# Decoding float64 weights in five vector operations, phi's maxima chunk by chunk, and a new plan table

## The chip, the cores and the metric

The kernel runs on one core of one Trainium2 chip. A core has five engines that run side by side, each with its own instruction list: PE (TensorE, matrix products into PSUM), DVE (VectorE), ACT (ScalarE), POOL (GpSimd) and SP (SyncE, which here only issues DMAs). The metric is the device time of one execution in microseconds (us).

## The reference

Attention with memory slots, then a feed-forward layer, all in float32:

```python
a = softmax(phi over the sequence)          # phi: 8 batches, 8 heads, 576 tokens, 32 slots
k_m = einsum('bhsm,bhsd->bhmd', a, k)       # keys and values gathered into the slots
v_m = einsum('bhsm,bhsd->bhmd', a, v)
attn = softmax(q @ k_m.T / 8 over the slots)
x = attn @ v_m                              # 4608 tokens x 512
h = x @ w_in                                # w_in 512 x 2048, w_out 2048 x 512
out = relu(h)**2 @ w_out
```

w_in and w_out arrive as float64, two 32-bit words for each number. The engines work in float32, so each weight has to be rebuilt from its words ("decoded").

## The kernel before, in words

**Products.** Every float32 product is made of several products of the rounded type fp32r: each operand is split into a high part (the value cast to fp32r) and a low part (what the cast left over), and PE adds high x high, high x low and low x high.

**Order of the mathematics.** The values of the slots are first multiplied with w_in (tiles `vw`), so h is made from the attention weights (`ath`, `atl`, high and low part) and `vw` in `mm1` (L1017). ACT and DVE make relu, square and the split (`gh`, `glo`), and `mm2` multiplies with the decoded w_out tiles `wo` (L1048 to L1051). Batches 0 and 1 are interleaved; they come first, and the weights are decoded while they run. From batch 5 on the second product runs in a form with seven products for eight (`fast`).

**The weight decode** (`decode`, L478 to L536) runs 32 times, 16 for w_in and 16 for w_out, each on 128 x 512 numbers: SP loads the raw words (`raw`, 512 KB, L494), DVE clamps the high word read as a float (L496), ACT scales it (L497), DVE takes the sign (L498), shifts and ORs (L499), masks the power (L500), multiplies the low word in (L512 or L514) and, for w_in, adds it (L516). Then ACT casts the high part (L411) and the low part is made by DVE (L529), or, for the first four decodes (`by_pe`), by PE with an identity matrix (`pd`, L522 to L524) and ACT (L527). For w_out beyond the first two, the low word's share is added to the low part by a DMA of POOL that accumulates (L533). w_in's parts are stored for later batches (L535).

**Slots** (`memory`): softmax of phi needs the maximum over 5 chunks of tokens (`mx`, L597, one reduce over a strided view of 128 x 640) and, from batch 2 on, the sum over them (`asum`, L626). PE turns it (`pmx`), then come subtraction, Exp and the products with k and v (`pkv`, L621).

**First attention** (`first_attention`, batches 0 and 1): q is turned by PE (`pq`, L882), multiplied with the keys (`psc`, L906), ACT copies the scores to `S`; the softmax is seven steps on DVE and ACT (`red` L953, L954, Exp, `rz` L956 to L958, L959); PE turns the result back (`pat`, L935), ACT casts `ath`, DVE makes `atl` (L939). Only then can `mm1` of that batch begin.

**What sets the order.** A planner in the kernel (`Plan`) lays every operation on an engine with given costs and writes all instruction lists out in advance; the engines then run them in that order and wait on semaphores. Its priorities are corrected, task by task, by the table `MOVED`. Where the plan leaves PE a gap between 18 and 90 us it puts in products that nobody reads (`idle`, L433).

Of the kernel before, what the change touches and what calls it, by code (L numbers as in the profile page):

```python
# [15 lines left out]
ALU = mybir.AluOpType  # L16
# [6 lines left out]
POWER = 0xFF800000  # L23
# [9 lines left out]
    2: 115, 6: -4, 11: 18, 13: -57, 22: 27, 26: 497, 32: 46, 34: 73, 44: -207, 48: 29, 50: 233, 60: 251, 62: 267,  # L33
    64: -163, 72: 276, 78: 503, 80: -141, 84: -49, 88: -48, 93: -8, 99: -20, 100: -414, 109: -99, 111: 31, 125: -273,
    127: -7, 129: 47, 135: -168, 143: -92, 151: -11, 157: 14, 159: -17, 161: -116, 163: -9, 167: -45, 169: -112,
    171: -28, 175: 15, 179: -58, 181: -141, 183: -217, 191: -27, 195: 39, 201: -208, 203: -184, 207: 15, 211: -137,
    215: 58, 217: 86, 237: 50, 240: 34, 244: -32, 246: -86, 248: -36, 250: -20, 252: -183, 256: -3, 258: 334, 268: 86,
    270: 177, 273: 131, 274: 35, 279: 90, 285: 24, 290: 52, 292: -438, 317: 292, 321: -449, 323: -13, 325: 16,
    327: -314, 329: -281, 340: 20, 363: -73, 365: -251, 367: 111, 370: 21, 386: -53, 389: 16, 394: -80, 402: -235,
    404: 32, 408: 34, 410: -307, 423: -17, 429: 7, 436: -380, 442: 35, 446: 228, 451: -824, 454: -102, 465: 207,  # L40
    467: 235, 481: 184, 539: 70, 543: 802, 554: -206, 557: 67, 575: 51, 586: 486, 587: 33, 612: -114, 616: -49,
    620: 111, 625: 155, 631: 128, 633: 25, 634: 118, 642: 42, 644: 125, 651: -12, 661: 62, 667: 43, 668: 58, 672: -64,
    674: 126, 678: 100, 680: 30, 687: 70, 694: -265, 698: 2, 702: 12, 713: 15, 717: 2, 743: -81, 762: 8, 765: 12,
    768: 171, 770: 47, 775: -132, 781: 58, 782: 50, 792: 43, 793: 94, 806: 33, 809: 19, 821: 8, 827: 84, 831: -47,
    836: -84, 841: -396, 847: -16, 853: -84, 858: 222, 859: -34, 860: -287, 864: -267, 865: 54, 872: 45, 880: 46,
    885: 331, 890: -17, 891: -245, 896: 23, 904: 344, 910: 41, 911: 198, 915: 27, 926: 419, 930: 216, 931: -134,
    936: -556, 941: 29, 958: -4, 964: 89, 977: 152, 1001: -155, 1005: 271,
# [293 lines left out]
def ts(n):  # L341
    return 65 + 0.52 * n
# [15 lines left out]
def tile_attention_moe(  # L358
# [120 lines left out]
    def decode(kind, j, h, room):  # L479
# [18 lines left out]
        vec({"DVE": ts(ND)}, lambda e: nc.vector.tensor_scalar(W(), high(), SIGN, None, ALU.bitwise_and), [rk], [wk], lead=True)  # L498
        vec({"DVE": tt(ND)}, lambda e: nc.vector.scalar_tensor_tensor(W(), T(), 3, W(), ALU.logical_shift_left, ALU.bitwise_or), [tk, wk], [wk], lead=True)  # L499
        vec({"DVE": ts(ND)}, lambda e: nc.vector.tensor_scalar(T(), W(), POWER, None, ALU.bitwise_and), [wk], [tk], lead=True)  # L500
# [7 lines left out]

        by_pe = j < 1
        late = kind == "wo" and not by_pe  # L510
        if by_pe:
            vec({"DVE": tt(ND)}, lambda e: nc.vector.scalar_tensor_tensor(part(1), low(), -2.0 ** -52, tf(), ALU.mult, ALU.mult), [rk, tk], [k1], lead=True)  # L512
        else:
            vec({"DVE": tt(ND)}, lambda e: nc.vector.scalar_tensor_tensor(tf(), low(), 2.0 ** -52, tf(), ALU.mult, ALU.mult), [rk, tk], [tk], lead=True)  # L514
            if not late:
                vec({"DVE": tt(ND)}, lambda e: nc.vector.tensor_add(wf(), wf(), tf()), [tk, wk], [wk], lead=True)  # L516
        op({"ACT": act(ND)}, lambda e: copy(e, part(0), wf()), [wk], [k0], lead=True)
        if by_pe:
            pd = pt("pv", f"pd{j}_{h}")

            def mm(e):
                nc.tensor.matmul(pd(), ident, wf(), start=True, stop=False)  # L522
                nc.tensor.matmul(pd(), minus, part(0), start=False, stop=False)
                nc.tensor.matmul(pd(), minus, part(1), start=False, stop=True)  # L524

            op({"PE": 1350}, mm, [wk, k1, k0], [pd], lead=True, lat=260)
            op({"ACT": acp(ND)}, lambda e: nc.scalar.copy(part(1), pd()), [pd], [k1], lead=True)  # L527
        else:
            vec({"DVE": tt(ND)}, lambda e: nc.vector.tensor_sub(part(1), wf(), part(0).bitcast(F32)),  # L529
                [wk, k0], [k1], lead=True)  # L530
        if late:

            dma(lambda d: d(out=part(1), in_=tf(), accum_op=ALU.add), [(2048 * P, 150)], [tk, k1], [k1], eng="POOL", lead=True)  # L533
# [38 lines left out]

    @plan.named
    def memory(b, hh, where=None):
# [21 lines left out]
        hm = lambda t: t().rearrange("p (h m) -> p h m", h=4)  # L596
        vec({"DVE": 1230}, lambda e: nc.vector.tensor_reduce(hm(mx), a().rearrange("p h c m -> p h m c"), AX.X, ALU.max), [A], [mx], lead=True)  # L597
        pm = pt("pa", f"pmx{u}")
        op({"PE": 60}, lambda e: nc.tensor.transpose(pm()[:, 0:P], mx(), ident), [mx], [pm], lead=True, lat=250, cold=200)
        mc = st([P, 1], F32, "mc", f"mc{u}")  # L600
        vec({"DVE": 210}, lambda e: nc.vector.tensor_reduce(mc(), pm()[:, 0:P], AX.X, ALU.max), [pm], [mc], lead=True)
        op({"PE": 60}, lambda e: nc.tensor.transpose(pm()[:, P:2 * P], mc().broadcast_to([P, P]), ident), [mc, pm], [pm], lead=True, lat=250, cold=200)
# [22 lines left out]
        if asum:  # L625
            vec({"DVE": 1250}, lambda e: nc.vector.tensor_reduce(hm(asum), a().rearrange("p h c m -> p h m c"), AX.X, ALU.add), [A], [asum], lead=True)  # L626
# [855 lines left out]
```

## Time and profile before

| | us |
|---|---|
| median of 3 runs | 761.42 |
| lowest and highest run | 760.92, 761.43 |
| span of the profiled execution | 757.5 |
| PE busy in the span | 735.3 |
| DVE busy in the span | 614.4 |

The times of the runs stand 3.9 us above the span, which runs from the first to the last recorded instruction; the profiled execution has no other time of its own in the records, so its own time is taken as span plus 3.9, the median. In the rows below, a line such as `48.83 0.40 PE L1017 ...` gives the start and the duration in us; what stands in square brackets is the idle time of the engine before it and what ended it. PE's matrix products overlap, so the distance from one start to the next is what a product takes from the engine, and its duration is longer.

### The profile page before, as it was taken

The page shows a single profiled execution, that of the slowest core. Times are in us where ns is not written, and L with a number is a line of the kernel's source. Part 1 is how long each engine was busy: PE and PEld are TensorE (multiplying, and loading weights), DVE is VectorE, ACT ScalarE, POOL GpSimd, SP SyncE. Part 2 cuts the span into 40 slices and gives each one's busy share as a digit, 9 for nine tenths or more (in the row PEclk, how much of TensorE's full clock was granted, in tenths as well). Part 3 has the DMA queues.
Part 4 walks back from the last instruction along what each step waited for, and adds up shares of the span by engine and source line. Part 5 has one row for each costly group of instructions (what it writes and reads, how often), then busy time and mean ns, then how long its engine had stood idle before and what let it go on. Part 6 is the DMA issues. An engine that isn't in the chain of part 4 may idle for free.

```text
span 757.5 us, 15358 instructions
## 1 busy us (share of the span) xinstructions
PE 735.3 (97%) x5535; PEld 651.8 (86%) x5535; DVE 614.4 (81%) x1478; ACT 436.1 (58%) x1000; POOL 74.2 (10%) x133
## 2 busy tenths in 40 slices
PE   4989999999999999999999999999999999999997
PEld 3767988888888888888888778888999999999997
DVE  5799998996679779977556675999989868987975
ACT  3666887875553555535445424767667545765752
POOL 4111111110101000001212221001000000000000
PEclk9999999999999999999999999999999999999999
DMA  8998997487765767544799687211766354544421
GB/s 261 328 300 228 282 283 208 161 227 202 212 166 166 204 195 197 167 110 120 276 369 312 205 259 242 64 32 33 191 161 178 90 135 132 161 119 154 140 71 42
DMA packets 84171, 139.85 MB, mean 185 GB/s; under 512 B 26592, under 2 KB 53216, under 8 KB 84096
## 3 DMA queue, kind: packets, MB, share of 16 engines
q1 hardware_dynamic: 68704, 102.59, 46.8%
q0 software_dynamic: 15296, 36.15, 15.2%
q8 instruction: 44, 0.72, 0.4%
q14 instruction: 31, 0.25, 0.1%
q10 hardware_dynamic: 96, 0.13, 0.1%
HBM read 100.34 MB, written 34.80 MB: 178 GB/s over the span
## 4 chain that ended last, share of the span: by engine, by line
PE 72%; DVE 9%; issue 8%; DMA 8%; ACT 1%; SPq 1%; POOL 0%; POOLq 0%; DVEq 0%; ACTq 0%
PE h L1017 11%; PE h L1155 9%; PE acc L1051 7%; PE acc L1048 7%; PE acc L1049 7%; PE accl L1267 3%; PE accl L1283 3%; PE psc L844 3%; DMA vw<-vw_kept 2%; PE pkv L621 2%; PE pvq_pv L786 2%; PE Mb L1212 1%; PE Mb L1213 1%; PE Mb L1215 1%; DMA kT_kept<-kT 1%
## 5 line engine op out<-in xcount | busy, mean ns | idle before, releaser
L1017 PE MATMUL h<-ath,vw 128*128 128x320 f32 (+1 forms) x640 | 132.8, 300 | 0.0
L1048 PE MATMUL acc<-wo,gh 128*128 128x512 f32 x320 | 129.3, 404 | 0.0
L1049 PE MATMUL acc<-wo,gh 128*128 128x512 f32 x320 | 125.9, 394 | 0.0
L1017 PEld LDWEIGHTS h<-ath,vw 128*128 128x128 f32 x640 | 104.1, 188 | 9.2 <-issue 0.6
L1051 PE MATMUL acc<-wo,glo 128*128 128x512 f32 x320 | 106.8, 405 | 0.7 <-DVE glo L1027 0.7
L1021 ACT ACTIVATE r<-h 128x320 f32<-128x320 f32 (+1 forms) x123 | 49.2, 409 | 59.9 <-PE h L1017 51.0
L1155 PE MATMUL h<-ath,vw 128*128 128x320 f32 (+1 forms) x384 | 78.1, 297 | 0.8 <-DMA vw<-vw_kept 0.8
L1051 PEld LDWEIGHTS acc<-wo,glo 128*128 128x128 f32 x320 | 58.5, 188 | 13.8 <-DVE glo L1027 1.6
L1048 PEld LDWEIGHTS acc<-wo,gh 128*128 128x128 f32 x320 | 60.3, 188 | 11.2 <-issue 0.6
L1049 PEld LDWEIGHTS acc<-wo,gh 128*128 128x128 f32 x320 | 60.2, 188 | 11.0
L1023 ACT ACTIVATE gh<-r 128x512 fp32r<-128x512 f32 x80 | 50.5, 631 | 33.2 <-DVE r L1022 15.9
L1017 PE MATMUL h<-atl,vw 128*128 128x256 f32 (+1 forms) x320 | 68.7, 295 | 0.1
L1027 DVE TENSOR_TENSOR glo<-r,gh 128x512 fp32r<-128x512 f32 x80 | 54.7, 685 | 12.4 <-ACT r L1025 6.4
L1155 PEld LDWEIGHTS h<-ath,vw 128*128 128x128 f32 x384 | 59.3, 188 | 1.7 <-PE h L1155 0.8
L1017 PEld LDWEIGHTS h<-atl,vw 128*128 128x128 f32 x320 | 51.3, 188 | 0.3 <-DVE atl L939 0.3
L1025 ACT ACTIVATE r<-r 128x576 f32<-128x576 f32 x67 | 45.8, 683 | 1.3
L411 ACT CAST vw<-pvw 64x512 fp32r<-64x512 f32 (+1 forms) x64 | 37.2, 581 | 14.7 <-PE pvw L753 12.1
L1183 ACT CAST H<-X 128x512 fp32r<-128x512 f32 x48 | 29.8, 620 | 20.0 <-DVE X L1176 10.3
L1155 PE MATMUL h<-atl,vw 128*128 128x256 f32 (+1 forms) x192 | 40.9, 294 | 0.0
L1184 DVE TENSOR_TENSOR LA<-X,H 128x512 fp32r<-128x512 f32 x48 | 32.6, 681 | 6.9 <-ACT H L1183 6.8
L761 DVE TENSOR_TENSOR vw<-pvw,vw 64x512 fp32r<-64x512 f32 x48 | 33.0, 687 | 2.5 <-ACT vw L411 1.3
L1155 PEld LDWEIGHTS h<-atl,vw 128*128 128x128 f32 x192 | 30.8, 188 | 0.0
(253 smaller groups left out, 1813.9 us busy)
## 6 DMA issues: line engine op xcount, KB each, us to landing
vw<-vw_kept SPq DMA_DIRECT2D x224, 128.0 KB, 3.7
wi<-w_in_kept SPq DMA_DIRECT2D x40, 512.0 KB, 4.3
vw_kept<-fold POOLq DMA_DIRECT2D x32, 512.0 KB, 5.4
KV<-in_v_dram SPq DMA_DIRECT2D x16, 512.0 KB, 5.2
raw<-in_moe_w_out_dram SPq DMA_DIRECT2D x16, 512.0 KB, 6.7
KV<-in_k_dram SPq DMA_DIRECT2D x16, 512.0 KB, 4.2
raw<-in_moe_w_in_dram SPq DMA_DIRECT2D x16, 512.0 KB, 8.0
w_in_kept<-wi POOLq DMA_DIRECT2D x16, 512.0 KB, 5.9
```

The lines of the kernel that those rows point to most:

```text
L411: nc.scalar.copy(o, i) if e == "ACT" else ENG[e].tensor_copy(o, i)
L761: vec({"DVE": 700}, lambda e, part=part, pr=pr: nc.vector.tensor_sub(part(1), pw()[pr], part(0).bitcast(F32)), [pw, (V, (0, hf))], [(V, (1 ...
L1017: nc.tensor.matmul(p()[:, 0:n], V()[:, l, hh, c0:c0 + P], x()[:, hh, cs], start=(i == 0), stop=(i == 5))
L1021: op({"ACT": act(n) - 40, **({} if b < 2 else {"DVE": tt(n)})}, lambda e, cs=cs, n=n, p=p: nc.scalar.activation(r()[:, cs], p()[:, 0:n], A ...
L1023: op({"ACT": act(SM)}, lambda e: nc.scalar.activation(gh(), r()[:, 0:SM], AF.Square), [r], [gh])
L1025: op({"ACT": act(S), **({} if b < 2 or b == FAST - 1 else {"DVE": tt(S)})}, lambda e: nc.scalar.activation(r(), r(), AF.Square) if e == "A ...
L1027: vec({"DVE": tt(SM)}, lambda e: nc.vector.tensor_sub(glo(), r()[:, 0:SM], gh().bitcast(F32)), [r, gh], [glo])
L1048: nc.tensor.matmul(a(), gh()[:, c], t()[:, 0], start=f0, stop=False)
L1049: nc.tensor.matmul(a(), gh()[:, c], t()[:, 1], start=False, stop=False)
L1051: nc.tensor.matmul(a(), glo()[:, c], t()[:, 0], start=False, stop=f1)
L1155: nc.tensor.matmul(p()[:, at:at + n], V()[:, l, hh, f0:f0 + P], x()[:, hh, cs], start=(i == 0), stop=(i == 5))
L1184: vec({"DVE": tt(w * P)}, lambda e, x=x, hi=hi, lo=lo: nc.vector.tensor_sub(lo().rearrange("p o f -> p (o f)"), x(), f32(hi())), src + [(H ...
```

## The change

`decode` now makes all its bits in one place. The low word times 2^-29, capped at 7, gives its three top bits; they are ORed with the sign, and with the shifted power and mantissa. The mask of the power, the product with the low word and the addition are gone, and so are the third PE product of the first four decodes and the accumulating DMAs of POOL. What the low word holds below its three top bits is no longer used. `fold` replaces both reduces of phi by four operations of 128 x 128 each. The table `MOVED` is new as a whole, and four planned PE costs differ, which changes the order on every engine.

```diff
 MOVED = {
-    2: 115, 6: -4, 11: 18, 13: -57, 22: 27, 26: 497, 32: 46, 34: 73, 44: -207, 48: 29, 50: 233, 60: 251, 62: 267,
...
+    1: -26, 5: -37, 6: -41, 7: 809, 11: 6, 13: -1331, 22: 90, 28: 949, 32: -525, 38: -297, 42: -80, 46: 227, 52: 1554,
...
-        vec({"DVE": ts(ND)}, lambda e: nc.vector.tensor_scalar(W(), high(), SIGN, None, ALU.bitwise_and), [rk], [wk], lead=True)
+        vec({"DVE": ts(ND)}, lambda e: nc.vector.tensor_scalar(W(), low(), 2.0 ** -29, 7.0, ALU.mult, ALU.min), [rk], [wk], lead=True)
+        vec({"DVE": tt(ND)}, lambda e: nc.vector.scalar_tensor_tensor(W(), high(), SIGN, W(), ALU.bitwise_and, ALU.bitwise_or), [rk, wk], [wk], lead=True)
         vec({"DVE": tt(ND)}, lambda e: nc.vector.scalar_tensor_tensor(W(), T(), 3, W(), ALU.logical_shift_left, ALU.bitwise_or), [tk, wk], [wk], lead=True)
-        vec({"DVE": ts(ND)}, lambda e: nc.vector.tensor_scalar(T(), W(), POWER, None, ALU.bitwise_and), [wk], [tk], lead=True)
...
-        if by_pe:
-            vec({"DVE": tt(ND)}, lambda e: nc.vector.scalar_tensor_tensor(part(1), low(), -2.0 ** -52, tf(), ALU.mult, ALU.mult), [rk, tk], [k1], lead=True)
-        else:
-            vec({"DVE": tt(ND)}, lambda e: nc.vector.scalar_tensor_tensor(tf(), low(), 2.0 ** -52, tf(), ALU.mult, ALU.mult), [rk, tk], [tk], lead=True)
-            if not late:
-                vec({"DVE": tt(ND)}, lambda e: nc.vector.tensor_add(wf(), wf(), tf()), [tk, wk], [wk], lead=True)
...
                 nc.tensor.matmul(pd(), ident, wf(), start=True, stop=False)
-                nc.tensor.matmul(pd(), minus, part(0), start=False, stop=False)
-                nc.tensor.matmul(pd(), minus, part(1), start=False, stop=True)
+                nc.tensor.matmul(pd(), minus, part(0), start=False, stop=True)
...
-        if late:
-            dma(lambda d: d(out=part(1), in_=tf(), accum_op=ALU.add), [(2048 * P, 150)], [tk, k1], [k1], eng="POOL", lead=True)
...
+    def fold(to, A, a, fn):
+        v = lambda: to().rearrange("p (h m) -> p h m", h=4)
+        for c in range(1, SC):
+            vec({"DVE": tt(P)}, lambda e, c=c: fn(v(), a()[:, :, 0] if c == 1 else v(), a()[:, :, c]), [A] + [to] * (c > 1), [to], lead=True)
...
-        vec({"DVE": 1230}, lambda e: nc.vector.tensor_reduce(hm(mx), a().rearrange("p h c m -> p h m c"), AX.X, ALU.max), [A], [mx], lead=True)
+        fold(mx, A, a, nc.vector.tensor_max)
...
-            vec({"DVE": 1250}, lambda e: nc.vector.tensor_reduce(hm(asum), a().rearrange("p h c m -> p h m c"), AX.X, ALU.add), [A], [asum], lead=True)
+            fold(asum, A, a, nc.vector.tensor_add)
```

**The first loads, on SP.** Here stands, of before, the end of batch 0's k and v (`KV_1`) with the first raw weights between them, and then q:

```order
L550 DMA KV_1_1_110<-in_v_dram 128x4x256
L551 DMA KV_1_1_110<-in_v_dram 64x4x64
L494 DMA raw<-in_moe_w_in_dram 128x2x512
L550 DMA KV_1_0_123<-in_k_dram 128x4x256
L551 DMA KV_1_0_123<-in_k_dram 64x4x64
L494 DMA raw<-in_moe_w_in_dram 128x2x512
L871 DMA q_0_156<-in_q_dram 128x4x256
L871 DMA q_1_189<-in_q_dram 128x4x256
L866 DMA qx_215<-in_q_dram 64x4x64
```

And here is the same place now:

```order
L543 DMA KV_1_0_108<-in_k_dram 128x4x256
L544 DMA KV_1_0_108<-in_k_dram 64x4x64
L543 DMA KV_1_1_118<-in_v_dram 128x4x256
L544 DMA KV_1_1_118<-in_v_dram 64x4x64
L869 DMA q_0_128<-in_q_dram 128x4x256
L869 DMA q_1_132<-in_q_dram 128x4x256
L864 DMA qx_135<-in_q_dram 64x4x64 x2
L499 DMA raw<-in_moe_w_out_dram 128x1024
L499 DMA raw<-in_moe_w_in_dram 128x2x512 x2
```

All of batch 0's k, v and q now go ahead of the first three raw weight tiles (one of w_out stood still earlier before).

**PE ahead of the first product of `mm1`.** Before, with `pmx_1` and `pvw_1_0` belonging to batch 1's slots and to the second weight slice:

```order
L935 MATMUL pat_1_639<-ident,S_1_459 128x128 x4
L942 MATMUL patl_646<-ident,S_1_459 128x128
L599 MATMUL pmx_1_651<-ident,mx_1_617 128x128
L733 MATMUL pvw_1_0_656<-wi_1_0_587,VTh_89 128x256 x4
L733 MATMUL pvw_1_0_656<-wi_1_0_587,VTl_93 128x256 x2
L733 MATMUL pvw_1_0_656<-wi_1_1_574,VTh_89 128x256 x4
L733 MATMUL pvw_1_0_656<-wi_1_1_574,VTl_93 128x256 x2
L1017 MATMUL h_0_677<-ath_603,vw_0_0_440 128x256 x2
```

Now, with `pvw_0_0` of the first slice and `pd_0` of the first w_out tile:

```order
L731 MATMUL pvw_0_0_462<-wi_0_1_424,VTh_91 128x256 x4
L731 MATMUL pvw_0_0_462<-wi_0_1_424,VTl_100 128x256 x2
L597 MATMUL pmx_0_484<-ident,mx_0_442 128x128
L438 MATMUL idle<-minus 128x512
L739 MATMUL pvw_0_0_462<-vw_0_0_487,minus 128x512
L933 MATMUL pat_1_495<-ident,S_1_404 128x128 x4
L940 MATMUL patl_502<-ident,S_1_404 128x128
L519 MATMUL pd_0_510<-work,ident 128x512
L520 MATMUL pd_0_510<-wo_366,minus 128x512
L600 MATMUL pmx_0_484<-ident,mc_0_505 128x128
L1015 MATMUL h_0_523<-ath_470,vw_0_0_487 128x256 x2
```

The second slice (`pvw_1_0`), batch 1's k and v products, their transposes, and one decode (`pd_1`) moved from in front of the first `mm1` to behind it.

**DVE during batch 0's softmax.** Before, from the first `red` of batch 0 (`S_0`), decode steps (`work`) and batch 1's `phi` stand between its steps:

```order
L953 TENSOR_REDUCE red_0_415<-S_0_402 128x16
L601 TENSOR_REDUCE mc_0_427<-pmx_0_417 128x1
L500 TENSOR_SCALAR work<-work 128x512
L954 TENSOR_TENSOR S_0_402<-S_0_402,red_0_415 128x512
L514 SCALAR_TENSOR_TENSOR work<-raw,work 128x512
L496 TENSOR_SCALAR work<-raw 128x512
L498 TENSOR_SCALAR work<-raw 128x512
L956 TENSOR_REDUCE rz_0_456<-S_0_402 128x16
L499 SCALAR_TENSOR_TENSOR work<-work 128x512
L603 TENSOR_TENSOR phi_0_225<-phi_0_225,pmx_0_417 128x640
```

Now:

```order
L951 TENSOR_REDUCE red_0_395<-S_0_384 128x16
L504 SCALAR_TENSOR_TENSOR work<-raw,work 128x512
L952 TENSOR_TENSOR S_0_384<-S_0_384,red_0_395 128x512
L505 SCALAR_TENSOR_TENSOR work<-work 128x512
L951 TENSOR_REDUCE red_1_421<-S_1_404 128x20
L954 TENSOR_REDUCE rz_0_426<-S_0_384 128x16
L952 TENSOR_TENSOR S_1_404<-S_1_404,red_1_421 128x640
L955 TENSOR_SCALAR rz_0_426<-rz_0_426 128x16
L570 TENSOR_TENSOR mx_0_442<-phi_0_221 128x128
L956 RECIPROCAL rz_0_426<-rz_0_426 128x16
L570 TENSOR_TENSOR mx_0_442<-mx_0_442,phi_0_221 128x128
L957 TENSOR_TENSOR S_0_384<-S_0_384,rz_0_426 128x512
```

The softmax steps of both halves now stand nearly side by side; from the first `red` to the last `atl` that `mm1` needs there are 4 decode steps of the two-tensor kind, 4 of the one-tensor kind, 8 softmax steps of full width, the 4 operations of one `fold`, 2 steps that make `atl`, and 5 short ones. `idle` products on PE: 17 before, 6 now.

## Rows read from the trace of the kernel before

**Rows 1.** The page: span, and busy time of each engine (share, count).
```profile
span 757.5 us, 15358 instructions
PE 735.3 (97%) x5535; PEld 651.8 (86%) x5535; DVE 614.4 (81%) x1478; ACT 436.1 (58%) x1000; POOL 74.2 (10%) x133
```

**Rows 2.** Windows: length, busy us by engine, granted clock, DMA share, GB/s.
```profile
20.00:40.00 20.00, 19.44 (x225) 14.37 (x225) 16.45 (x37) 13.04 (x26) 2.19 (x6) 1.00 1.08 319
40.00:60.00 20.00, 16.77 (x162) 13.05 (x160) 20.00 (x46) 12.65 (x31) 3.91 (x6) 1.00 1.02 302
60.00:400.00 340.00, 337.61 (x2416) 287.73 (x2408) 278.34 (x585) 202.09 (x439) 39.70 (x71) 1.00 0.70 209
400.00:757.50 357.50, 351.63 (x2507) 329.94 (x2505) 287.85 (x783) 202.46 (x497) 20.37 (x34) 1.00 0.49 142
```

**Rows 3.** Waits of PE from 60 us on: total us, times, longest.
```profile
PE pmx L599 <- DVE mx L597: 1.2, 3, 0.5
PE h L1155 <- DMA vw<-vw_kept: 0.8, 2, 0.5
```

**Rows 4.** Timeline of PE, 0 to 62 us.
```profile
19.28 1.11 PE L621 MATMUL pkv<-KV,phi 128*32 128x64 f32 x25 [0.84 <-issue]
20.32 0.47 PE L657 MATMUL pvt<-ident,kvx 128*128 128x128 f32 x1
...
23.98 1.03 PE L882 MATMUL pq<-ident,q 128*128 128x128 f32 x8
24.85 0.27 PE L657 MATMUL pkt<-ident,kvx 128*128 128x128 f32 x1
...
26.73 1.90 PE L906 MATMUL psc<-kbd,qT 128*128 128x64 f32 x16
28.46 0.61 PE L882 MATMUL pq<-ident,q 128*128 128x128 f32 x4
...
35.57 0.60 PE L633 MATMUL pkv<-ones,phi 128*32 128x1 f32 x40
36.50 1.12 PE L522 MATMUL pd<-work,ident 128*128 128x512 f32 x2 [0.33 <-ACT wo L527]
...
38.03 1.73 PE L621 MATMUL pkv<-KV,phi 128*32 128x64 f32 x80
...
47.02 1.02 PE L733 MATMUL pvw<-wi,VTh 128*128 128x256 f32 x4
...
48.83 0.40 PE L1017 MATMUL h<-ath,vw 128*128 128x256 f32 x2
...
57.80 0.60 PE L633 MATMUL pkv<-ones,phi 128*32 128x1 f32 x40 [0.75 <-ACT phi L605]
```

**Rows 5.** Timeline of DVE, 0 to 62 us.
```profile
19.88 0.43 DVE L496 TENSOR_SCALAR work<-raw 128x512 f32<-128x512 f32 x1 [0.57 <-DMA raw<-in_moe_w_in_dram]
...
29.28 0.69 DVE L953 TENSOR_REDUCE red<-S 128x16 f32<-128x512 f32 x1 [0.61 <-ACT S L911]
...
31.07 0.68 DVE L514 SCALAR_TENSOR_TENSOR work<-raw,work 128x512 f32<-128x512 uint32 x1
31.67 0.42 DVE L496 TENSOR_SCALAR work<-raw 128x512 f32<-128x512 f32 x1
32.01 0.42 DVE L498 TENSOR_SCALAR work<-raw 128x512 uint32<-128x512 uint32 x1
...
33.54 0.81 DVE L603 TENSOR_TENSOR phi<-phi,pmx 128x640 f32<-128x640 f32 x1
34.27 0.71 DVE L500 TENSOR_SCALAR work<-work 128x512 uint32<-128x512 uint32 x1
...
44.00 1.22 DVE L597 TENSOR_REDUCE mx<-phi 128x128 f32<-128x640 f32 x1
45.12 0.83 DVE L959 TENSOR_TENSOR S<-S,rz 128x640 f32<-128x640 f32 x1
```

**Rows 6.** DVE's groups by line and shape: busy us, mean ns, idle before.
```profile
L1176 DVE TENSOR_TENSOR X<-XD,X 128x128 f32<-128x128 f32 x48 | 13.5, 282 | 0.0
```

## What the change will do to the time

> **What bounds the kernel now.** I read the busy times first: PE is busy 735.3 of 757.5 us, DVE 614.4 [rows 1]. So the time is PE's work plus the time in which PE has none. The stretches say where that is: 0.6 us idle from 20 to 40, 3.2 from 40 to 60, then 2.4 in 340 us, and 5.9 in the last stretch [rows 2], of which most is the evacuation and store behind the last product. PE's own waits from 60 us on make six lines of 3.7 us together; the two longest stand in [rows 3]. Saving DVE work after 60 us can therefore give back 3.7 us at the very most.
>
> The start is different. PE gets its first `mm1` product at 48.83 [rows 4]; up to there it has little real work, and 15 of the 17 `idle` products stand there and count as busy. DVE is full from 40 to 60 (20.00 of 20.00, [rows 2]), and the first `mm1` hangs on batch 0's softmax, which crosses DVE from 29.28 to behind 45.12 [rows 5]. So the question is when `mm1` begins now, and how much real work PE has by then.
>
> **The decode.** Before, on DVE: a one-tensor step takes 0.34 us from start to start (31.67 to 32.01), a two-tensor step 0.60 (31.07 to 31.67) [rows 5]. Of w_in from the second slice on there were 3 of the one and 4 of the other, 3.4 us; now 2 and 3, 2.5. The w_out tiles go from 2.8 to 2.5, the first four from 2.2 to 1.9. In sum 14 x 0.9 + 14 x 0.3 + 4 x 0.3 = 18 us less on DVE, of which nearly all lies beside busy PE and is worth nothing by itself. The new first step reads integers, calculates in float and writes integers, which no row shows: 0.34 if it goes like the other one-tensor steps, 0.60 if like a two-tensor step. I take 0.34, the nearest row (same widths, same strided input); the other end costs 0.8 on the path below, since three of them stand in it. The four third products of `pd` vanish from in front of `mm1`, where PE waits anyway; the accumulating DMAs vanish from POOL, which holds up nobody on PE in these rows.
>
> **The fold.** The reduce takes 1.12 from start to start (44.00 to 45.12) [rows 5]. Its four successors take 0.28 each [rows 6], and each needs the one before, so 1.13 back to back: no gain. If other instructions stand between them they overlap and cost less, which bounds the gain at about 0.3 for each of 28 folds, under other work; if a dependent start costs extra, they lose as much. I take nothing.
>
> [...]
>
> **The start, worked out.** *Where the softmax begins.* Before, the last part of batch 0's k starts on PE at 19.28 and takes 1.11 [rows 4]. In the new SP order two raw tiles (1.05 MB) no longer stand ahead of it: at 319 GB/s [rows 2] it is 3.3 us earlier, so this ends at 17.1. Then PE has 19 transposes (16 of q) and `psc_0`. Eight transposes take 0.87 (23.98 to 24.85), `psc` 1.73 (26.73 to 28.46) [rows 4], but a single transpose lasted 0.47 at 20.32 and 0.27 at 24.85: up to about 24 us PE runs at what looks like the lower of its two levels. With everything doubled until 24, the transposes end at 21.2 and `psc_0` at 24.4. From the end of `psc` to `red` it was 0.8 (28.46 to 29.28): 25.2. For q's landing and the copies of q^T, which now follow at once, I add 0.7: `red` at 25.9, against 29.28 before. From the other side, the second raw tile of w_in was used at 19.88 [rows 5]; four q loads (1.18 MB, 3.7 us) now go ahead of it: 23.6, and three decode steps later DVE is free at 24.9. So 25.9 stands, and 24.9 to 27.5 bounds it.
>
> *How long it takes.* On DVE, in the order shown, up to the last `atl`: 4 x 0.60 and 4 x 0.34 of the decode, 4 softmax steps of 512 at 0.60 and 4 of 640 at 0.73 (33.54 to 34.27), 4 x 0.28 of the fold, 2 x 0.60 for `atl`, and five short ones, 0.7 as an estimate: 2.4 + 1.4 + 2.4 + 2.9 + 1.1 + 1.2 + 0.7 = 12.1. The waits on ACT's Exp and on `pat` fit between, with other steps filled in. `mm1` begins at 38.0; I allow 0.5 for hand-overs and take 38.5 (37.4 to 41.0).
>
> *What is moved behind it.* Durations of before [rows 4]: sums of batch 1's slots 0.60, one `pd` 1.2 (36.50 to 38.03 less its third product), k and v 1.73, three transposes 0.8, `pvw_1_0` 1.8 (47.02 to 48.83): 6.1, less 0.4 of overlap and pauses, 5.7. So the old start of 48.83 compares with 43.1, and the gain at this point is 4.6 us.
>
> *What comes late next.* After `mm1` begins, PE needs in turn `wi` of the second slice, batch 1's Exp and the second pair of w_out tiles, each made on DVE a microsecond or less ahead, by the same counting. Before, PE lost 0.75 at 57.80 [rows 4]. I put 1.0 in its place. Past 60 us the order is much like before's, and I leave the 3.7 us. Sum: 761.4 - 4.6 + 0.3 = 757.1, made against the profiled execution's span plus 3.9, which is the median of the runs.
>
> **Rivals.**
> 1. *The clock falls (slower).* In the new order PE has, between `pd_0` at some 26 us and 38.5, only about 7.5 us of work, and 6 idle products instead of 17. [...] Against it: the granted clock reads 1.00 from 20 to 60 [rows 2], through gaps with few products. [...] I give it 0.08. [...]
> 2. *The raw tiles come late.* With q and batch 1's phi, k and v ahead of them, the fourth and fifth raw tile land only about as DVE wants them (33 to 34 us). If the DMAs are a tenth slower, `mm1` waits up to 3 us: 41.5, and the time is 760.1, at the edge of no change. 0.14.
> 3. *The rest of the plan loses it.* Every task is re-timed. If PE's waits past 60 us rise from 3.7 to 8, the time is 761.4. The order there looks alike, which speaks against it. 0.10.
> 4. *More than that.* No hand-over lost, `mm1` at 37.4, and half of the later waits gone, since DVE has 18 us less to do: 761.4 - 5.7 - 1.9 = 753.8. 0.10.
> 5. *The new step isn't cheap.* At 0.60 it costs 8 us of DVE in all but 0.8 on the path: 757.9. It stays within the forecast, which gets 0.58 with it.
>
> **How the numbers follow.** 757.1 is the forecast's centre, and its own range is 755 to 759.5. Taking in most of rivals 2, 3 and 4 gives 753.6 to 761.6; about 0.2 is left outside, with rival 1. A measurement here tells 0.2%, or 1.5 us, from no change: faster is below 759.9. That is the forecast (0.58), rival 4 (0.10) and half of rival 2: 0.75. No change takes the other half of 2 and half of 3: 0.13. Slower takes rival 1 and what of 3 goes further: 0.12.
>
> **What the profile of the changed kernel would show.** The first `red` near 26, the first `mm1` product between 37.4 and 41, PE busy behind it with waits of about 1 us up to 60; the new first decode step at 0.42 us duration like its neighbours; a fold of four spanning about 1.1; PE's waits past 60 us near 3.7; the granted clock at 1.00 from 24 us on. I am wrong if `mm1` starts later than 42, if a stretch shows a half clock, or if PE's waits past 60 us reach 8.

## The result, and the profile after

| | before | after |
|---|---|---|
| median, us | 761.42 (760.92 to 764.69, 4 runs) | 751.60 (751.30 to 752.03, 4 runs) |
| span of the profiled execution, us | 757.5 | 749.7 |

The ratio is 0.9865, 95% interval 0.9833 to 0.9898: 9.8 us faster, where 4.3 were forecast; the time lies 2.0 us below the range. First the page of after: the span, and busy time of each engine. It answers to [rows 1].

```profile
span 749.7 us, 15337 instructions
PE 730.3 (97%) x5520; PEld 650.8 (87%) x5520; DVE 593.4 (79%) x1533; ACT 427.8 (57%) x983; POOL 62.0 (8%) x119
```

Next the windows of after (columns as in [rows 2]) and PE's waits from 60 us on, which answer to [rows 3].

```profile
20.00:40.00 20.00, 18.75 (x110) 15.29 (x111) 18.63 (x47) 14.69 (x31) 2.12 (x5) 1.00 1.07 339
40.00:60.00 20.00, 20.00 (x280) 16.72 (x283) 18.96 (x49) 17.10 (x38) 1.89 (x4) 1.00 0.90 298
60.00:400.00 340.00, 338.88 (x2459) 290.34 (x2448) 264.27 (x635) 196.62 (x431) 31.17 (x62) 1.00 0.66 204
400.00:749.70 349.70, 342.84 (x2446) 321.83 (x2444) 284.26 (x781) 196.32 (x481) 18.78 (x30) 1.00 0.49 140
```

```profile
PE pmx L597 <- DVE mx L570: 1.1, 1, 1.1
PE Mc L1210 <- ACT H L1181: 0.9, 1, 0.9
PE h L1153 <- DMA vw<-vw_kept: 0.7, 1, 0.7
PE pvq_pa L784 <- DVE fold L793: 0.5, 1, 0.5
```

**Where the 7.8 us of span went.** PE's busy time fell by 5.0 us, its idle time by 2.8 (22.2 to 19.4). Idle time, window by window: unchanged up to 20 us, 0.7 more from 20 to 40, 3.2 less from 40 to 60 (PE is now busy for 20.00 of 20.00), 1.3 less from 60 to 400, 1.0 more in the last stretch. Of the busy time, 3.6 us are `idle` products: 17 before, in groups of 0.99, 0.62, 0.98, 0.71, 1.64 and 0.62, and 6 now, in groups of 1.09, 0.40 and 0.48. The four third products of `pd` are 1.1: three add 0.24 each, and the first, still at the slower pace, 0.42. 0.3 I can't assign.

The same can be put as one number: PE's busy time up to 60 us without the `idle` and the third products. That leaves 39.4 us of work before and 46.6 after, so at 60 us the new kernel is some 7.2 us ahead. Nearly all of the gain is made in the first 60 us.

The timeline of PE in after, for [rows 4], and of DVE, for [rows 5]:

```profile
18.93 1.02 PE L619 MATMUL pkv<-KV,phi 128*32 128x64 f32 x24 [1.50 <-issue]
...
20.15 1.91 PE L880 MATMUL pq<-ident,q 128*128 128x128 f32 x8
...
23.99 2.46 PE L904 MATMUL psc<-kbd,qT 128*128 128x64 f32 x16
...
32.91 0.66 PE L933 MATMUL pat<-ident,S 128*128 128x128 f32 x4 [0.56 <-DVE S L957]
...
38.05 0.48 PE L1015 MATMUL h<-ath,vw 128*128 128x256 f32 x2
...
38.93 0.39 PE L1015 MATMUL h<-atl,vw 128*128 128x256 f32 x1 [0.28 <-DVE atl L937]
```

```profile
24.93 0.42 DVE L503 TENSOR_SCALAR work<-raw 128x512 uint32<-128x512 uint32 x1
...
27.11 0.69 DVE L951 TENSOR_REDUCE red<-S 128x16 f32<-128x512 f32 x1 [0.82 <-ACT S L909]
...
38.20 0.67 DVE L937 TENSOR_TENSOR atl<-pat,ath 128x512 fp32r<-128x512 f32 x1
```

`red` starts at 27.11 (29.28 before), the first `mm1` product at 38.05 (48.83 before).

**The base of the sum.** Every later execution comes with its own span. In all of them the time is the span plus 1.7 to 1.8 us, in those of e7 plus 1.8 to 2.1. The profiled execution of before, with its 757.5, was therefore one of some 759.2 us, not 761.4. Over 82 executions before has a median of 761.8 us and a median span of 760.1; 6 had a span of 757.5 or less. So 2 us of the 9.8 are the distance of that one execution from its median.

### The profile page after: what moved, and what is told of

Its sections match the earlier page's. It is cut to its first block, busy times and chain, and to the rows that moved or that the text cites. A ratio compares the mean times of both kernels' runs of the same rounds, so it can differ in the third digit from the quotient of the medians.

```text
span 749.7 us, 15337 instructions
## 1 busy us (share of the span) xinstructions
PE 730.3 (97%) x5520; PEld 650.8 (87%) x5520; DVE 593.4 (79%) x1533; ACT 427.8 (57%) x983; POOL 62.0 (8%) x119
## 4 chain that ended last, share of the span: by engine, by line
PE 91%; DMA 3%; DVE 3%; SPq 1%; issue 1%; ACT 0%; ACTq 0%
PE h L1015 17%; PE acc L1046 10%; PE acc L1049 10%; PE h L1153 10%; PE acc L1047 10%; PE accl L1265 3%; PE psc L842 3%; PE pkv L619 3%; PE accl L1281 2%; PE pvw L751 2%; DMA vw<-vw_kept 2%; PE pvq_pv L784 2%; PE Mb L1210 1%; PE Mb L1211 1%; PE Ma L1210 1%; PE Ma L1211 1%
## 5 line engine op out<-in xcount | busy, mean ns | idle before, releaser
L1015 PE MATMUL h<-ath,vw 128*128 128x256 f32 (+1 forms) x640 | 130.0, 299 | 0.0
L1049 PE MATMUL acc<-wo,glo 128*128 128x512 f32 x320 | 113.5, 408 | 0.0
L1153 PE MATMUL h<-ath,vw 128*128 128x256 f32 (+1 forms) x384 | 79.6, 298 | 0.8 <-DMA vw<-vw_kept 0.7
L1047 PEld LDWEIGHTS acc<-wo,gh 128*128 128x128 f32 x320 | 60.2, 188 | 10.5
L1015 PE MATMUL h<-atl,vw 128*128 128x320 f32 (+1 forms) x320 | 68.7, 295 | 0.3 <-DVE atl L937 0.3
L1019 ACT ACTIVATE r<-h 128x320 f32<-128x320 f32 (+1 forms) x122 | 47.8, 407 | 29.6 <-PE h L1015 16.4
L1023 ACT ACTIVATE r<-r 128x576 f32<-128x576 f32 x64 | 43.4, 683 | 1.2
L1181 ACT CAST H<-X 128x512 fp32r<-128x512 f32 x48 | 29.6, 618 | 25.3 <-PE Ma L1211 14.1
L1153 PE MATMUL h<-atl,vw 128*128 128x256 f32 (+1 forms) x192 | 41.0, 295 | 0.0
```

The costliest lines, as they stand in the source:

```text
L1015: nc.tensor.matmul(p()[:, 0:n], V()[:, l, hh, c0:c0 + P], x()[:, hh, cs], start=(i == 0), stop=(i == 5))
L1019: op({"ACT": act(n) - 40, **({} if b < 2 else {"DVE": tt(n)})}, lambda e, cs=cs, n=n, p=p: nc.scalar.activation(r()[:, cs], p()[:, 0:n], A ...
L1023: op({"ACT": act(S), **({} if b < 2 or b == FAST - 1 else {"DVE": tt(S)})}, lambda e: nc.scalar.activation(r(), r(), AF.Square) if e == "A ...
L1047: nc.tensor.matmul(a(), gh()[:, c], t()[:, 1], start=False, stop=False)
L1049: nc.tensor.matmul(a(), glo()[:, c], t()[:, 0], start=False, stop=f1)
L1153: nc.tensor.matmul(p()[:, at:at + n], V()[:, l, hh, f0:f0 + P], x()[:, hh, cs], start=(i == 0), stop=(i == 5))
```

## The experiments

| | kernel | median, us | ratio to before (95%) |
|---|---|---|---|
| e1 | old order, new decode | 760.23 | 0.9989 (0.9968 to 1.0010) |
| e2 | the same and the fold | 760.81 | 0.9989 (0.9973 to 1.0004) |
| e3 | new order, old VectorE work | 779.17 | 1.0231 (1.0207 to 1.0254) |
| e4 | new order, reductions | 756.17 | 0.9929 (0.9910 to 0.9947) |
| e5 | e1 without fillers | 759.47 | 0.9948 (0.9916 to 0.9980) |
| e6 | new order, 14 accumulating DMAs | 786.35 | 1.0310 (1.0257 to 1.0362) |
| e7 | after, empty table | 765.44 | 1.0041 (1.0007 to 1.0074) |
| e8 | before, empty table | 769.96 | 1.0098 (1.0068 to 1.0128) |
| e9 | after, raw tiles ahead of q | 753.83 | 0.9916 (0.9888 to 0.9944) |
| e10 | after, ten late DMAs | 769.73 | 1.0105 (1.0076 to 1.0134) |
| e11 | after, one pmx later | 751.78 | 0.9876 (0.9854 to 0.9898) |
| e12 | after, no fillers | 753.57 | 0.9897 (0.9876 to 0.9917) |
| e13 | e10, another source | 759.74 | 0.9964 (0.9931 to 0.9997) |
| e14 | e6, another source | 773.23 | 1.0153 (1.0079 to 1.0226) |
| e15 | after, one step more per decode | 759.45 | 0.9953 (0.9921 to 0.9984) |

After itself was run on one occasion only. Before was run beside the experiments on each, with medians of 761.42 (e1 to e4), 762.20 (e5 to e8), 760.92 (e9 to e12) and 762.49 (e13 to e15). So a difference from after of some 1.5 us can't be told from the occasion.

**e1 and e2, the new work in the old order.** The new steps stand in the places of the old ones; the PE list is that of before but for the four third products, and SP's is word for word the same.

```diff
-tensor_scalar(W(), high(), SIGN, None, ALU.bitwise_and)
+tensor_scalar(W(), low(), 2.0 ** -29, 7.0, ALU.mult, ALU.min)
...
+scalar_tensor_tensor(W(), high(), SIGN, W(), ALU.bitwise_and, ALU.bitwise_or)
 scalar_tensor_tensor(W(), T(), 3, W(), ALU.logical_shift_left, ALU.bitwise_or)
-tensor_scalar(T(), W(), POWER, None, ALU.bitwise_and)
...
-dma(lambda d: d(out=part(1), in_=tf(), accum_op=ALU.add), ...)
```

> The order of before on every engine; the decode's five VectorE operations stand in the places of its seven (32 third operations of it fewer, the third subtraction product at four preparations and the 14 accumulating transfers gone); phi's maxima and sums stay single reductions. Theory A (the new table's order gains nearly all of the 9.8 us, the removed work little): within 1.5 us of before, 760 to 761.4 us, and TensorE's wait for mx in front of pmx, the two in the first 40 us included, as before. Theory B (the removed VectorE and GpSimd-queue work gains it, since it feeds TensorE just in time): at least 4 us faster, 757.5 us or less, in the old order. By the working of the prediction (0.9 us of TensorE's products gone, some VectorE time ahead of TensorE's waits at the start): 758.5 to 760.5 us.

e2 makes the fold in place as well:

```diff
-tensor_reduce(hm(mx), a().rearrange("p h c m -> p h m c"), AX.X, ALU.max)
+for c in range(1, SC): tensor_max(hm(mx), a()[:, :, 0] if c == 1 else hm(mx), a()[:, :, c])   # asum likewise, with add
```

> As the run before it, and phi's maxima and sums chunk by chunk in the places of the single reductions, still in the order of before. Theory A: 759.5 to 761.4 us, the four short operations take about as long as one reduction. Theory B: 755 us or less. If the chunk-by-chunk form shortens the wait in front of pmx, each of 16 waits loses at most 0.3 us, so at most 1.5 us below the run before it.

760.23 and 760.81: no change clear of the noise (the interval of e1 reaches from 2.4 us faster to 0.8 slower), which rules out theory B. DVE is busy for 599.7 us in e1 instead of 614.4, and little or nothing comes of it. The trace shows where it goes. The first `mm1` product starts 1.6 us earlier than before, but then PE waits for `atl`, which the old order makes late (0.89 us), and from the product at 50.65 on (50.70 before) nothing is left of it:

```profile
47.26 0.40 PE L1016 MATMUL h<-ath,vw 128*128 128x256 f32 x2
...
48.66 0.39 PE L1016 MATMUL h<-atl,vw 128*128 128x256 f32 x1 [0.89 <-DVE atl L938]
```

**e3 and e4, the old work in the new order.** Now every list is that of after, with the old number of VectorE operations in the decode and for phi (e3; the transfers of POOL stay out), or only with one reduction in place of each fold (e4).

```diff
 scalar_tensor_tensor(W(), T(), 3, W(), ALU.logical_shift_left, ALU.bitwise_or)
+tensor_scalar(T(), W(), 0, None, ALU.bitwise_and)
+scalar_tensor_tensor(tf(), low(), 2.0 ** -52, tf(), ALU.mult, ALU.mult)   # w_in from the second slice on
...
-for c in range(1, SC): tensor_max(v(), a()[:, :, 0] if c == 1 else v(), a()[:, :, c])   # e3 and e4
+tensor_reduce(v(), a().rearrange("p h c m -> p h m c"), AX.X, ALU.max)
```

> The order of after on every engine, with the VectorE work of before put back into it: one 128x512 tensor_scalar more in every decode and one 128x512 scalar_tensor_tensor more in the decodes of w_in after the first preparation (both write a buffer nobody reads afterwards), and single reductions for phi's maxima and sums. Some 20 us more of busy VectorE. Theory A: 751.5 to 753.5 us, TensorE's waits beyond 60 us at most 5 us in sum. Theory B: 755 us or more, since VectorE then comes late for TensorE.

> After with single tensor_reduce instructions for phi's maxima and sums, in the order of after; nothing else changed. Theory A: 751 to 752.5 us. Theory B: 752.5 us or more. If four short operations cost more VectorE time than one reduction, it may be up to 0.5 us faster than after; the wait in front of pmx at 306 us (1.1 us in after) tells which form ends earlier.

Theory A falls as hard as theory B did: e3 is 27.6 us slower than after, and 18 slower than before. The new order with the old VectorE work is far worse than the old one. It also has 17 operations on DVE that the old order had on ACT, and its DVE is busy for 622.7 us, against 614.4 in before. The longest waits of PE past 60 us, and the window of 60 to 160 us, where PE has 10.5 us without work and the granted clock averages 0.97 (1.00 in after):

```profile
PE acc L1051 <- DVE glo L1027: 4.0, 3, 2.3
PE h L1017 <- ACT r L1021: 2.6, 2, 1.7
PE pkv L636 <- DVE asum L572: 1.9, 3, 0.8
```

```profile
60.00:160.00 100.00, 89.47 (x625) 76.38 (x626) 94.02 (x195) 68.51 (x147) 6.93 (x13) 0.97 0.62 203
```

e4 is 4.6 us slower than after. It doesn't lose this at the start (its first `mm1` product is at 37.50, after's at 38.05); from 60 to 400 us PE is idle for 3.1 us instead of 1.1, and the rest isn't assigned. For the fold [rows 6] are answered by these groups of DVE (busy us, mean ns), the first two of e4, the others of after:

```profile
L570 DVE TENSOR_REDUCE mx<-phi 128x128 f32<-128x640 f32 x16 | 20.8, 1299 | 5.7 <-DMA phi<-in_phi_dram 3.9 <-DMA kT_kept<-kT 1.3 <-issue 0.5
L570 DVE TENSOR_REDUCE asum<-phi 128x128 f32<-128x640 f32 x12 | 15.7, 1306 | 2.1 <-ACT phi L603 2.0
```

```profile
L570 DVE TENSOR_TENSOR mx<-mx,phi 128x128 f32<-128x128 f32 x48 | 14.5, 303 | 1.5
L570 DVE TENSOR_TENSOR mx<-phi 128x128 f32<-128x128 f32 x16 | 4.7, 294 | 5.2 <-DMA phi<-in_phi_dram 2.9 <-DMA KV<-in_k_dram 1.3 <-PE pmx L597 0.6
```

A reduction lasts 1.30 us, and DVE is busy 6.8 us longer with 28 of them (600.2 against 593.4). The short operations that stand for a maximum last 0.29 to 0.30 us each, and four of them keep DVE busy for 1.20 (14.5 + 4.7 over 16), so here they are the cheaper form.

**e5, the old order without fillers.** e1, all else in the same order:

```diff
-FILL = 18000, 90000
+FILL = 0, 0
```

> The old order with the new decode (the first experiment, 760.2 us), and the 17 filler products that the written order holds between 18 and 60 us left out; they take 5.6 us of TensorE there, beside 2.0 us for after's six. Theory C (freed VectorE time cannot show in the old order since fillers stand where the old waits were): 755 to 758 us, the start up to the first mm1 product 2 to 4 us earlier. Theory D (the old order's sequence itself, not its fillers, holds the work back: the fillers only cover waits that would be there anyway): within 1 us of the first experiment, the fillers' time turned into waits of the same length. If the clock falls without them, slower than 762 us with a granted clock of 0.5 somewhere before 60 us.

759.47, 0.8 us less than e1, or 1.5 less when each is set against before on its own occasion. The time of the fillers turns into waits, as theory D says: `pat` now waits 1.85 us, since the step of DVE that it needs (L958) starts at 43.32 as against 43.59 in e1. And the granted clock falls, to 0.66 from 40 to 50 us and to 0.50 from 43 to 49, with no wait longer than that:

```profile
40.00:50.00 10.00, 6.68 (x33) 5.72 (x31) 9.79 (x22) 4.94 (x13) 1.07 (x2) 0.66 1.07 347
43.00:49.00 6.00, 4.80 (x23) 4.74 (x24) 5.84 (x13) 2.60 (x5) 0.53 (x1) 0.50 1.06 359
```

```profile
44.20 1.11 PE L934 MATMUL pat<-ident,S 128*128 128x128 f32 x4 [1.85 <-DVE S L958]
...
48.09 0.63 PE L1016 MATMUL h<-ath,vw 128*128 128x256 f32 x2
```

From this `pat` to the first `mm1` product it is 3.89 us, against 2.71 in e1 at 1.00, so `mm1` comes later and not 2 to 4 us earlier, as theory C has it. So the old sequence itself keeps PE without work there. The 3.6 us of fillers that after saves are no cause of the gain; in the old order they stand where waits would be, and the granted clock from 40 to 60 us reads 1.00 with them (e1) and 0.83 without (e5).

**e6, the accumulating DMAs in the new order.** After, with the 14 transfers issued behind `wo`'s low part:

```diff
-tensor_sub(part(1), wf(), part(0).bitcast(F32))
+(tensor_sub(part(1), wf(), part(0).bitcast(F32)), nc.gpsimd.dma_start(out=part(1), in_=tf(), accum_op=ALU.add))   # w_out, j >= 1
```

> After, with the 14 accumulating transfers of before back on GpSimd's queue (256 KB each, onto the same part of w_out; what they add is the scaled value of the scratch tile, practically zero). Theory: they lie off the path in the new order as in the old, 751.3 to 752.8 us. Rival (GpSimd's queue or the 16 DMA engines are short of time in the new order): 754 us or more, with TensorE's waits named after wo.

786.35: 34.8 us more than after, for transfers whose removal gained nothing in e1. The first such tile shows it. In before its low part is made at 52.00, the transfer is issued at 53.01, and PE first uses the tile at 65.92 (DVE, POOL and PE of before; which product is a tile's first is taken from the written instruction lists):

```profile
52.00 0.70 DVE L529 TENSOR_TENSOR wo<-work,wo 128x512 fp32r<-128x512 f32 x1
...
53.01 0.90 POOL L533 DMA_DIRECT2D wo<-work  x1 [4.12 <-DVE wo L529]
...
65.92 0.40 PE L1048 MATMUL acc<-wo,gh 128*128 128x512 f32 x1
```

After uses it 0.3 us behind its last step:

```profile
53.78 0.68 DVE L525 TENSOR_TENSOR wo<-work,wo 128x512 fp32r<-128x512 f32 x1
...
54.76 0.40 PE L1046 MATMUL acc<-wo,gh 128*128 128x512 f32 x1
```

With the transfer back (e6) PE stands for 7.59 us at the product with the low part, and its next products take 0.63 instead of 0.40:

```profile
52.95 0.69 DVE L525 TENSOR_TENSOR wo<-work,wo 128x512 fp32r<-128x512 f32 x1
...
53.96 0.39 PE L1046 MATMUL acc<-wo,gh 128*128 128x512 f32 x1
...
54.20 0.90 POOL L525 DMA_DIRECT2D wo<-work  x1 [6.85 <-ACT wo L416]
...
61.94 0.80 PE L1047 MATMUL acc<-wo,gh 128*128 128x512 f32 x1 [7.59 <-DMA wo<-work]
62.53 0.63 PE L1046 MATMUL acc<-wo,gh 128*128 128x512 f32 x1
```

Over all 14 tiles, the time from the last step to the first use is 7.3 us or more in before, where a transfer takes 6.2 us (median); in after the first four tiles have 0.3, 6.3, 7.5 and 1.5 us.

**e7 and e8, without a table.** In after and in before:

```diff
-MOVED = { ... }
+MOVED = {}
```

> The code of after with an empty table, so that the planner's own due times set the order. Theory E (the table carries the gain: without it the freed VectorE time is worth little): 757 to 775 us, and no more than 3 us from the code of before with an empty table. Theory F (the removed work pays by itself once the planner plans for it): at least 5 us faster than the code of before with an empty table.

> The code of before with an empty table, the partner of the run before it: 762 to 778 us. Theory E: at most 3 us slower than after's code without its table. Theory F: at least 5 us slower than it.

765.44 and 769.96: 4.5 us between them, in the gap between the two theories. Neither holds as it stands, and with e7's runs between 763.04 and 769.45 both are possible at their edges. By these medians the change is worth 4.5 us when it is planned anew by the same rules; the other 5.3 of the 9.8 come from the table, which is worth 13.8 us to after and 8.5 to before. Whether a better table for before exists wasn't tried, so how much of the 5.3 belongs to the removed work stays open. Much of the early start is there without a table, as the first `mm1` product of e7, then of e8 shows (48.83 in before, which is faster than e8, so this start alone doesn't decide):

```profile
40.44 0.39 PE L993 MATMUL h<-ath,vw 128*128 128x256 f32 x2
```

```profile
46.05 0.40 PE L1001 MATMUL h<-ath,vw 128*128 128x256 f32 x2
```

**e9, q's place in SP's queue.** After, with the first three raw tiles issued ahead of batch 0's q.

```diff
+early = the first three raw loads in the written order
-for o in plan.order():
+for o in (the order, with early moved to just before the first q load):
     o.fn(o.left)
```

> After, with one thing of before's SP queue put back: the first three raw weight tiles (1.6 MB) are issued ahead of batch 0's four q loads, where after has them behind. All other queues as in after. Theory (the place of q in the SP queue is what starts the softmax earlier, as the prediction says): the first red 2 to 3.5 us later than in after's profile (27.1), the first mm1 product likewise behind 38.05, and the time 753.5 to 755 us. Rival (the transposes in front of psc wait for PE's and the copies' pace, not for q): red within 0.5 us, time 751.3 to 752.3 us.

```profile
28.66 0.69 DVE L953 TENSOR_REDUCE red<-S 128x16 f32<-128x512 f32 x1
```

```profile
22.44 1.97 PE L882 MATMUL pq<-ident,q 128*128 128x128 f32 x8 [2.09 <-DMA q<-in_q_dram]
...
39.60 0.48 PE L1017 MATMUL h<-ath,vw 128*128 128x256 f32 x2
```

753.83, 2.2 us more than after: PE now waits 2.09 us for q, `red` comes at 28.66 (1.55 later) and `mm1` at 39.60 (1.55 later). The 2.2 us alone are little more than the occasions differ by; the trace shows that q's place in the queue acts on `red` and `mm1`, at about half of the size expected.

**e10, the ten late transfers.** As e6, but:

```diff
-nc.gpsimd.dma_start(out=part(1), in_=tf(), accum_op=ALU.add)   # w_out, j >= 1
+nc.gpsimd.dma_start(out=part(1), in_=tf(), accum_op=ALU.add)   # w_out, j >= 3
```

> As the run with 14 accumulating transfers in the new order (786.4 us), but only the ten of the w_out tiles from the fourth slice on are put back; the four of the second and third slice stay out. In after's trace the ten tiles are first used 9.6 to 52 us behind their decode, those four 0.3, 6.3, 7.5 and 1.5 us. Theory (a transfer costs what of its some 6 us does not fit into the tile's slack): 751.3 to 754 us. Rival (GpSimd's queue and the DMA engines are what is short): 770 us or more, ten fourteenths of the 35 us.

769.73: neither theory. The ten tiles have slack enough, and still the transfers cost 18.1 us. DVE shows one reason: while a transfer reads the scratch tile `work`, the next decode can't write it, and what stands behind that decode in DVE's list (`glo`) waits too. A wait of DVE from 40 to 220 us in e10, the timeline of DVE at another, and the window that follows there (granted clock 0.50):

```profile
DVE work L503 <- DMA wo<-work: 2.4, 1, 2.4
```

```profile
115.03 0.42 DVE L501 TENSOR_SCALAR work<-raw 128x512 f32<-128x512 f32 x1
118.38 0.43 DVE L503 TENSOR_SCALAR work<-raw 128x512 uint32<-128x512 uint32 x1 [2.93 <-issue]
118.72 0.69 DVE L1025 TENSOR_TENSOR glo<-r,gh 128x512 fp32r<-128x512 f32 x1
```

```profile
120.00:125.00 5.00, 5.00 (x18) 4.53 (x17) 3.92 (x7) 3.20 (x10) 0.00 (x0) 0.50 0.24 68
```

The profile names the transfer for the 2.4 us but no releaser for the 2.93, so there the scratch is an inference; e13 tests it. Part of the 18.1 us is the clock, as this window shows.

**e13 and e14, another source.** The transfers read `part(0)` of their own tile, which no decode waits for.

```diff
-nc.gpsimd.dma_start(out=part(1), in_=tf(), accum_op=ALU.add)
+nc.gpsimd.dma_start(out=part(1), in_=part(0).bitcast(F32), accum_op=ALU.add)
```

> As the run with ten late accumulating transfers (769.7 us), but they read the tile's own upper part and not the decode's scratch tile (so that w_out there counts about double in the output). Theory S (the transfer holds the scratch, and the next decode waits for it on VectorE): 751.3 to 754 us, and VectorE's waits at the first decode step gone. Theory Q (the transfers load GpSimd's queue and the DMA engines): 765 us or more, as before.

> The same with all 14 transfers (786.4 us with the scratch as their source). Theory S: the four early tiles are used 0.3 to 7.5 us behind their decode, so TensorE still waits some 5 us each at two or three of them, and the clock may fall behind these: 760 to 772 us, with the waits of acc on wo as the longest. Theory Q: 780 us or more.

Ten transfers cost 8.1 us (759.74) instead of 18.1, so holding the scratch was some 10 of them, the clock that fell behind the waits included; the time lies between the two theories. DVE no longer waits for `wo<-work`, but up to 1.9 us for a raw tile of w_in (the profiled execution is the longest of ten, 763.43). The rest stays with transfers whose source no decode waits for; whether it is the queue, the DMA engines or the clock (0.99 from 60 us on in e13, 0.98 from 60 to 400 in e10) stays open. The four early ones add 13.5 us (773.23, 1.2 above theory S's range), and PE's wait for them is about that of e6, where the same line reads 14.5 us, 2 times, 7.6 at most:

```profile
PE acc L1047 <- DMA wo<-wo: 14.6, 2, 8.2
```

**e15, one step more.** After, in each of the 32 decodes:

```diff
 scalar_tensor_tensor(W(), T(), 3, W(), ALU.logical_shift_left, ALU.bitwise_or)
+tensor_scalar(T(), W(), 0, None, ALU.bitwise_and)
```

> After with one 128x512 tensor_scalar more in each of the 32 decodes (11 us of VectorE in all, on a buffer nobody reads afterwards), the order unchanged. If each step counts only where VectorE is on the path up to mm1 (three decodes, 1.0 us) and hides elsewhere: 752 to 754 us. If the new order is tight throughout the prepared slices: 757 us or more, with TensorE waiting for wi and wo tiles up to 160 us.

759.45: the additional steps, 12.6 us of busy VectorE (606.0 against 593.4), cost 7.9. None of it is lost up to `mm1`, which starts at 38.03 as in after. From 60 to 160 us, while the later slices are decoded, PE in after has no idle time at all, and in e15 3.2 us. The time is that of the second case, but not its sign: PE's waits there are for `glo` (0.7), `S` (0.7 and 0.5) and others, none for a `wi` or `wo` tile. Windows of after, then of e15:

```profile
60.00:160.00 100.00, 100.00 (x682) 89.02 (x671) 93.62 (x199) 82.23 (x176) 7.97 (x14) 1.00 0.67 227
```

```profile
60.00:160.00 100.00, 96.81 (x668) 83.25 (x659) 96.93 (x211) 78.68 (x167) 7.87 (x14) 1.00 0.64 217
```

**e11 and e12, faster still?** e11 changes PE's list around the `pmx` that waits 1.1 us at 306 us; e12 is after with `FILL = 0, 0`, as in e5. The list of e11, in short:

```diff
-pmx (maximum), acc, acc, pmx (its broadcast), acc, acc      # each acc a pair of products
+acc, acc, pmx (maximum), acc, acc, pmx (its broadcast)
```

> After, with four w_out products (two pairs) ahead of the one pmx transpose that waits 1.1 us for the fold at 306 us, and two pairs ahead of its partner; nothing else moved. Theory (PE's waits past 60 us are time lost one for one): 0.7 to 1.1 us faster than after, 750.5 to 751 us, and no pmx line among PE's waits. Rival (the stall moves on, since what follows on VectorE is late as well): within 0.3 us of after.

> After without its six filler products (2.0 us of TensorE between 29 and 36 us). Theory C (fillers stand in the way of work that is ready): 0.3 to 1.5 us faster, 750 to 751.3 us, with the clock at 1.00. Rival (they fill waits that are there anyway, as in the old order, where leaving out 5.6 us of them gained about 1): within 0.3 us. If the clock drops to half in front of mm1, as the 0.83 from 40 to 60 us in the old order without them suggests, 1 to 4 us slower.

751.78 and 753.57. e11 is within 0.2 us of after: its `pmx` wait is down from 1.1 to 0.5, but PE's wait lines past 60 us sum to 3.6 against 3.2, so other waits took its place. In e12 the clock stays at 1.00 and PE is full from 40 to 60 us as in after; its profile loses time late instead (PE waits 1.4 for `vw` and 1.0 for `H`), far from the six products taken out, and the runs of after were not taken beside these, so I don't call it slower. Neither beats after.

## Why the prediction was wrong

**Right.** The direction, and the place: the start. `mm1` at 38.05 was forecast as 38.5, `red` at 27.11 lies between its bounds, the first decode step takes 0.42 like its neighbours, PE's waits past 60 us are 3.2. So rivals 2 (no raw tile held up `mm1`), 3 and 5 are out. Rival 1 is out as well. The granted clock reads 1.00 from 20 us on, which alone would not settle it, since the column reads 1.00 also from 20 to 25 us, where eight `pq` take 1.91 us (1.03 in before at 23.98); but `pat` and `pvw` ahead of `mm1` take 0.66 and 0.72 as in before. e5 shows such a fall in the old order (0.50 from 43 to 49 us). What one would have cost in the new order no run shows; in e5 the way from `pat` to the first `mm1` product took 1.2 us more (3.89 against 2.71). Rival 4 named a time (753.8) near the result; its first half came (no hand-over lost), its second, half of the later waits gone, did not. e9 shows q's place in the queue at work.

**Partly luck: `mm1`.** Misses cancel. The last products for batch 0's slots were to end on PE at 17.1, 3.3 us earlier than before; they ended at 19.95, 0.4 earlier. From there to `red` it took 7.2 us and not 8.8, so `red` came 1.2 later than forecast. From `red` DVE took 11.8 us to the end of the last `atl` (12.1 forecast), but `mm1` needs only `ath` for its first products: it began 0.8 ahead of that end and not 0.5 behind it.

**Wrong, 1: the base of the sum.** "The profiled execution's span plus 3.9, which is the median of the runs" set one execution's profile against the median of others. Its own time was some 759.2. That is 2.0 of the 5.5 us missed.

**Wrong, 2: the terms at and behind `mm1`.** The 5.7 us of work moved behind `mm1` were 4.7: without `idle` and third products PE is busy for 29.6 us ahead of `mm1` before, and for 24.9 now. "I put 1.0 in its place" was 1.0 us of hand-over for 0.75. From `mm1` to 60 us PE waited for 0.28 us in all, where before it lost 0.82 in gaps and 0.62 in fillers: 1.4 us more than forecast. With `mm1` 0.45 earlier, the lead at 60 us is 7.2 and not 4.3, which is 2.9 of the 5.5. Past 60 us, PE's idle time fell by 1.3 us up to 400 and rose by 1.0 behind it, where I left all as it was; that and the 0.3 that I can't assign are the rest.

**Wrong, 3: why it is worth that.** This step adds nothing to the 5.5 us; it is the one that failed in kind. The prediction priced the edits one by one on the rows of before: the 18 us of DVE "worth nothing by itself", the DMAs that hold up "nobody on PE in these rows", the fold at nothing. All three are true of the old order, within the noise (e1, e2). In the new one they are its condition: putting the operations of the decode and the reductions back (e3) costs 27.6 us, one short step in each decode 7.9 (e15), the reductions alone 4.6 (e4), the transfers 34.8 (e6). The terms don't add up, since each is measured with the others gone, and those of e3 and e6 contain stretches at a lower clock (0.97 from 60 to 160 us in e3, 0.64 from 60 to 70 in e6). Before had 13 us between its first such w_out tile and the tile's first use, twice what a transfer takes (6.2, median); after has 0.3, and with a transfer there PE stands for 7.59 us (e6). That the new table made its gain out of this room is my reading; no run tests it alone.

**My own theories.** "The order pays" and "the work pays" both fell. What the runs support: neither does alone (e1 and e3), and by the medians of e7 and e8 4.5 us come from planning the smaller work by the same rules.

**Open.** The 0.3 us of PE's busy time; why batch 0's slot products ended only 0.4 us earlier; how good a table for before could be; why the executions of before spread from 757 to 768 us while four of after lie within 0.7; how the 8 us of e13 divide between queue, DMA engines and clock.

## What to carry to other kernels

Where the order of all engines is written in advance, an edit that removes work is worth what the new order makes of the room, so it is not priced on the rows of the old one: look for slack that the removed work had forced (from a tile's last step to its first use, the time that a scratch tile stays held), and count it as something that can be had. Test order and work apart, each with the other kept. And make the sum against the time of the same execution as the profile, not against the median of others.

## What the hardware showed beyond that

The accumulating DMAs of 256 KB (6.2 us from issue to landing in before, 5.0 in e6, medians) held up what needed their target (PE stands for 7.59 us in e6) and what needed their source (some 10 of 18 us in e10 against e13). What is left with a free source, the 8 us of e13, isn't divided.

The PE stop of 7.59 us in e6 cost more than its length: the granted clock reads 0.85 from 50 to 60 us and 0.64 from 60 to 70, and though PE resumes at 61.94, the 512-wide products of `acc` last 0.63 us or more up to the one that starts at 66.59; the one at 67.33 lasts 0.40. The stretch behind the stop:

```profile
60.00:70.00 10.00, 8.06 (x105) 6.21 (x109) 4.46 (x10) 2.58 (x4) 0.56 (x1) 0.64 0.24 74
```

In e5, too, the clock fell, to 0.50 from 43 to 49 us, with waits of 1.85 us at most and products between them. So in e6 it fell around one long stop, and in e5 among several short waits (0.79, 0.68 and 1.85 us); what sets it off the two don't settle. After, whose longest wait of PE past 20 us is 1.1, shows 1.00 from there on.
